# A gated-state recurrence with a mixture of experts behind it: the last chunk's first layer by 44 for 48 matmuls, the state decay as one operation, two experts of chunk 1's first half by seven products

## The chip, the cores and the metric

The kernel runs on one core of one Trainium2 chip, as one launch. The metric is the device time of an execution in microseconds (us). A core has a matrix engine (PE, TensorE; its weight loads are listed as PEld), a vector engine (DVE), an activation engine (ACT), a general engine (POOL, GpSimd) and a queue that issues transfers (SP). Each works through its own list in order. Matmuls write to PSUM, which has eight banks of 128 x 512 f32.

## The reference

```python
f = 1 / (1 + exp(-f_logit))                    # q, k, v, f_logit: 4 batches, 8 heads, 768 steps, 48 wide
for t in range(S):
    state = f[:, :, t, :, None] * state + einsum('bhd,bhe->bhde', k[:, :, t], v[:, :, t])
    y[:, :, t] = einsum('bhd,bhde->bhe', q[:, :, t], state)
x = y.transpose(0, 2, 1, 3).reshape(3072, 384)
p = domain_probs / (domain_probs.sum(-1, keepdims=True) + 1e-9)
for e in range(4):
    h = maximum(x @ w1[e], 0)                  # 384 -> 1024
    out += p[:, e:e+1] * (h @ w2[e])           # 1024 -> 384
```

## The kernel before

The 768 steps are cut into six chunks of 128 (`c` = 0 to 5). In each chunk the recurrence becomes, per batch `b`, a masked product of queries and keys plus a product with the state carried over; the chunk's 4 x 128 rows then go through the four experts. All matmuls are in bf16 with f32 sums.

**The experts.** In chunk 0 and the first half (batches 0 and 1) of chunk 1 each expert is done by itself: `add_h` makes columns of the hidden layer (`mm_h`, L492: three matmuls of 128 x 128 weights for 128 hidden columns) and `relu` takes them out of PSUM; `add_o` makes an output tile from eight matmuls of 384 columns per batch (`mm_o`, L507). From the second half of chunk 1 on, experts go in pairs `p` for two batches at a time (a half `hf`): `mm_hs` (L524, 256 columns) makes the hidden layer with the row probabilities already multiplied into x, since they are not negative, and `relu_s` (L530 on DVE, L532 on ACT) takes it out, 512 columns at a time. The second layer of a pair is done by seven products instead of eight (Strassen's scheme in Winograd's form): the hidden block is cut into 2 x 2 parts (rows by batch, columns by half), `s_sum` (L547) makes four sums of parts, `t_sum` (L569) four sums of the weights, and `mm_p` (L583) makes the seven products of eight matmuls of 192 columns. Products 1, 6, 7 and 4 are added up in one bank X, 5 and 3 in a bank Y, 2 alone in Z; after each step of X the partial result is read out, so X goes on only when the read is done (`ev_p`, L610 on DVE, copies L281 on ACT). Experts for which `BLOCKED` holds are done in the same way one by one (`mm_p1`, L591; `ev_p1`, L599); before, that is expert 1 in chunks 0 and 1.

**The state.** After each batch of a chunk but the last, `ev_kv` (L471, DVE) adds the new outer products to `Sf`, and `state` (POOL) multiplies `Sf` by the gate (L479) and casts it to bf16 (L476). The 96 state rows lie as two blocks of 48 in partitions 0 to 47 and 64 to 111, and before each block has an operation of its own: two products and two casts per batch and chunk.

**The order.** The whole program is a list of named operations. `Plan.add` gives each a rank from the table `RANKS` (one number per operation, with a letter where two engines could do it: A for ACT, D for DVE, P for POOL), and the operations are issued in the order of their ranks; each engine's list follows from that. PSUM banks and SBUF slots (`rooms`) are given out in the same order. An operation on POOL whose name begins with q, k, v, s or t (products, casts, sums) waits for the last DVE operation of that kind ahead of it in the order (`o.turn`).

Of the kernel before, what the change touches and what calls it, by code (L numbers as in the profile page):

```python
# [139 lines left out]
def kernel(  # L140
# [11 lines left out]
    nc = tc.nc  # L152
# [814 lines left out]

    for e in BLOCKED:
        t_sums(e)
# [97 lines left out]
```

## Time and profile before

| | |
|---|---|
| median of 3 runs | 288.09 us (287.63 to 289.83) |
| profiled execution | 290.13 us, its span 288.4 us, mean granted clock 0.988 |
| busy PE / PEld / DVE / ACT / POOL | 278.3 / 240.1 / 205.8 / 166.0 / 110.2 us |
| chain that ended last | PE 92%, DMA 5%, POOL 1%, SP 1% |
| transfers | 41.87 MB, mean 145 GB/s |

Busy times can't be added up: the engines work side by side. A PE that is shown as busy need not be full, since the end of a matmul is modelled with what it still takes to leave the array; how many matmuls there are in how much time says more. The chain that ended last is followed back from the last instruction, at each step to what released it; its pieces have a start, a length and the engine with the line. Rows of waits say which engine's line sat idle until which other operation ended.

### The profile page before, as it was taken

What the parts mean: (1) busy time and instruction counts of PE and PEld (TensorE: products, weight loads), DVE (VectorE), ACT (ScalarE), POOL (GpSimd) and SP (SyncE); (2) the same over time, 40 slices, a digit from 0 to 9 for tenths busy, and PEclk for the clock granted to TensorE, in tenths of its full rate; (3) what the DMA queues carried; (4) which work ended last, traced back from release to release, by engine and by line L of the source; (5) the groups of instructions that cost most, each with busy time, mean ns of one, the idle gap of its engine ahead of it and who ended that gap; (6) DMA issues with size and microseconds to landing.
All of it is one profiled execution on the core that took longest, in us unless ns stands there. A gap on an engine that the chain in (4) does not pass through costs nothing.

```text
span 288.4 us, 7572 instructions
## 1 busy us (share of the span) xinstructions
PE 278.3 (96%) x3056; PEld 240.1 (83%) x3056; DVE 205.8 (71%) x435; ACT 166.0 (58%) x326; POOL 110.2 (38%) x186
## 2 busy tenths in 40 slices
PE   6769999999999999999999999999999999999995
PEld 3549556668787998998998999998999999999995
DVE  4855576797778888856768857767578868666474
ACT  5745525848777885757768738754735434613510
POOL 5997200406496614756466552534022111000000
PEclk9977999999999999999999999999999999999999
DMA  7999999998997999989999999964930642220003
GB/s 159 199 198 208 206 193 190 188 197 163 166 174 147 200 204 187 186 165 187 209 189 185 168 203 195 172 128 91 142 91 0 97 109 55 57 56 1 30 0 113
DMA packets 153687, 41.87 MB, mean 145 GB/s; under 512 B 144028, under 2 KB 152860, under 8 KB 153652
## 3 DMA queue, kind: packets, MB, share of 16 engines
q1 hardware_dynamic: 142404, 34.66, 64.7%
q0 software_dynamic: 11248, 6.72, 16.5%
q8 instruction: 24, 0.39, 0.6%
q14 instruction: 11, 0.09, 0.1%
HBM read 31.51 MB, written 4.72 MB: 126 GB/s over the span
## 4 chain that ended last, share of the span: by engine, by line
PE 92%; DMA 5%; POOL 1%; SPq 1%; issue 0%; DVE 0%
PE ps_m L524 33%; PE ps_m L583 29%; PE ps_m L492 12%; PE ps_m L507 8%; DMA w_sb<-in_moe_w_dram 3%; PE ps_m L591 2%; PE ps_m L431 2%; PE ps_m L458 2%; DMA k<-in_k_dram 1%; PE ps_m L454 1%; PE ps_m L341 1%; PE ps_m L464 1%; POOL vb L287 1%; SPq L293 1%; PE ps_m L483 0%; PE ps_m L400 0%
## 5 line engine op out<-in xcount | busy, mean ns | idle before, releaser
L524 PE MATMUL ps_m<-x,w_sb 128*128 128x256 bf16 x864 | 107.4, 273 | 0.0
L532 ACT ACTIVATE h<-ps_m 128x512 bf16<-128x512 f32 x105 | 59.5, 602 | 63.3 <-PE ps_m L524 56.1
L524 PEld LDWEIGHTS <-w_sb 128*128 128x128 bf16 x864 | 82.3, 98 | 8.6
L583 PEld LDWEIGHTS <-S 128*128 128x128 bf16 x576 | 48.7, 98 | 1.5
L610 DVE TENSOR_TENSOR o<-ps_m,o 128x192 f32<-128x192 f32 x91 | 31.3, 353 | 23.9 <-PE ps_m L583 22.4
L492 PE MATMUL ps_m<-x,w_sb 128*128 128x128 bf16 (+2 forms) x264 | 37.5, 295 | 2.0 <-DMA w_sb<-in_moe_w_dram 2.0
L583 PEld LDWEIGHTS <-h 128*128 128x128 bf16 x432 | 36.5, 98 | 0.6
L530 DVE TENSOR_SCALAR h<-ps_m 128x512 bf16<-128x512 f32 x39 | 26.7, 687 | 12.4 <-PE ps_m L524 12.0
L414 ACT ACTIVATE yb<-ps_m,pn 128x384 bf16<-128x384 f32 x59 | 31.6, 589 | 5.3 <-PE ps_m L458 3.7
L479 POOL TENSOR_TENSOR Sf<-Sf,egs 48x192 f32<-48x192 f32 x40 | 20.2, 507 | 35.5 <-DVE S L547 18.6
L492 PEld LDWEIGHTS <-w_sb 128*128 128x128 bf16 x264 | 23.4, 105 | 10.2 <-DMA w_sb<-in_moe_w_dram 2.1
L503 ACT ACTIVATE h<-ps_m 128x512 bf16<-128x512 f32 (+1 forms) x42 | 20.8, 507 | 15.6 <-PE ps_m L492 14.6
L583 PE MATMUL ps_m<-ts_sb,S 128*128 128x192 bf16 x288 | 29.5, 246 | 0.0
L583 PE MATMUL ps_m<-w_sb,h 128*128 128x192 bf16 x288 | 29.3, 246 | 0.0
L583 PE MATMUL ps_m<-w_sb,S 128*128 128x192 bf16 x288 | 29.2, 246 | 0.0
L391 POOL TENSOR_TENSOR qk<-q,e 128x384 bf16<-128x384 f32 x19 | 22.6, 1190 | 13.8 <-issue 4.9
L547 DVE TENSOR_TENSOR S<-h 128x1024 bf16<-128x1024 bf16 x36 | 25.6, 716 | 2.9 <-ACT h L532 2.6
L507 PE MATMUL ps_m<-w_sb,h 128*128 128x384 bf16 x144 | 27.0, 326 | 0.0
L447 DVE TENSOR_TENSOR AT<-ps_m,mask 128x512 bf16<-128x512 f32 x40 | 25.6, 682 | 1.0 <-PE ps_m L431 0.9
L374 ACT ACTIVATE e<-ps_m 128x384 f32<-128x384 f32 x40 | 23.8, 713 | 3.3 <-PE ps_m L341 3.2
L476 POOL CAST sb<-Sf 48x192 bf16<-48x192 f32 x40 | 14.0, 354 | 24.8 <-DVE S L547 14.7
L391 POOL TENSOR_TENSOR qk<-k,e 128x384 bf16<-128x384 f32 x19 | 18.9, 999 | 11.7 <-PE ps_m L464 7.8
(97 smaller groups left out, 336.7 us busy)
## 6 DMA issues: line engine op xcount, KB each, us to landing
out_dram<-o SPq DMA_DIRECT2D x23, 192.0 KB, 2.5
w_sb<-in_moe_w_dram POOLq DMA_DIRECT2D x5, 768.0 KB, 17.3
q<-in_q_dram SPq DMA_DIRECT2D x10, 384.0 KB, 5.4
k<-in_k_dram SPq DMA_DIRECT2D x10, 384.0 KB, 5.2
v<-in_v_dram SPq DMA_DIRECT2D x10, 384.0 KB, 5.6
f<-in_f_logit_dram SPq DMA_DIRECT2D x9, 384.0 KB, 5.3
w_sb<-in_moe_w_dram POOLq DMA_DIRECT2D x6, 384.0 KB, 9.9
f<-in_f_logit_dram SPq DMA_DIRECT2D x6, 192.0 KB, 4.0
```

The lines of the kernel that those rows point to most:

```text
L374: nc.scalar.activation(out=o, in_=i, func=AF.Exp, scale=1.0 if j else -1.0)
L391: return engines[eng].tensor_tensor(out=tl("qk", c, b)[:, j, :, 0:D].rearrange("t (i r) d -> t i r d", r=2), in0=tl("qk"[j], c, b // 2)[:, ...
L414: nc.scalar.activation(out=ys, in_=y, func=AF.Copy, scale=pe)
L447: nc.vector.tensor_tensor(out=tl("AT", c, b)[:, r].rearrange("s i t -> s (i t)"), in0=tl("A", c, b, r).rearrange("s i t -> s (i t)"), in1= ...
L492: nc.tensor.matmul(out=hp(c, e, fc, n0, n1, nf)[:, f], lhsT=w1_sb[:, e, kk, (fc + f) * 128:(fc + f + 1) * 128], rhs=tl("xT", c)[:, kk, n0: ...
L507: nc.tensor.matmul(out=tl("op", c, e, nt)[:, 0:Din], lhsT=tl("h", c, e, half_of(c, nt * T))[:, fc, nt * T:(nt + 1) * T], rhs=w2_sb[:, e, f ...
L524: nc.tensor.matmul(out=out_[:, f], lhsT=w1_sb[:, e, kk, (fc + f) * 128:(fc + f + 1) * 128], rhs=tl("xs", c, hf, p)[:, el, kk, :], start=(k ...
L530: nc.vector.tensor_relu(out=dst, in_=tl("hp", c, hf, p, el, fc))
L532: nc.scalar.activation(out=dst, in_=tl("hp", c, hf, p, el, fc), func=AF.Relu)
L547: return nc.vector.tensor_tensor(out=o, in0=in0, in1=in1, op=op)
L583: nc.tensor.matmul(out=out_, lhsT=lhs[:, f, :], rhs=rhs[:, f, :], start=(first and el == 0 and f == 0), stop=(el == 1 and f == KH - 1), sk ...
L610: nc.vector.tensor_tensor(out=o, in0=src, in1=o, op=ALU.add)
```

## The change

1. `LOW` names all four groups (half, pair) of the last chunk. For each expert of such a group `l1_unit` makes the first layer by a seven-product scheme of its own. The first 256 of the 384 inputs by the 1024 hidden columns by the 256 rows is cut 2 x 2 x 2; the third block of 128 inputs is added to those products that end in one result each. A step makes four hidden blocks by 128 rows, 512 columns of a bank: steps 1, 6 and 7 of 4 matmuls, steps 2, 5, 3 and 4 of 8, each of 128 columns; 44 in all, where `mm_hs` has 24 of 256 columns, that is 48 such. Only the first matmul of a bank clears it. Steps 1, 6, 7, 4 share a bank X as above. Steps 2, 5 and 3 are copied by ACT into SBUF (`copy_l1`), and the hidden parts are made on DVE by an addition with a maximum against 0 (`ev_l1`), the last one on ACT alone.
2. The scheme needs five sums of first-layer weights per expert (`u_sum`) and four sums of inputs per group (`x_sum`), on DVE or POOL, in SBUF slots that the last loads have left.
3. The state decay is one operation on 112 rows (chunks 1 to 4), and decays and casts may stand on DVE or ACT too.
4. `BLOCKED` takes in expert 3 of chunk 1. In chunk 1's first half two hidden blocks of 256 columns share a bank and one eviction (`hl`).
5. `s_sum`, `s_sum1` and `t_sum` may stand on POOL. `RANKS` is new throughout.

```diff
+    def u_sum(e, j, eng):
+        a = lambda i, kk: wblk(e, i, kk)
+        in0, in1, op = {1: lambda: (a(1, 0), a(1, 1), ALU.add), 2: lambda: (usum(e, 1), a(0, 0), ALU.subtract),
+                        3: lambda: (a(0, 0), a(1, 0), ALU.subtract), 4: lambda: (a(0, 1), usum(e, 2), ALU.subtract),
+                        5: lambda: (a(0, 2), a(1, 2), ALU.subtract)}[j]()
+        return engines[eng].tensor_tensor(out=usum(e, j), in0=in0, in1=in1, op=op)
...
+        terms = {"1": lambda: [(wblk(e, 0, 0), x(0, 0))], "2": lambda: [(wblk(e, 0, 1), x(1, 0)), (wblk(e, 0, 2), x(2, 0))],
+                 "5": lambda: [(usum(e, 1), t(1)), (wblk(e, 1, 2), x(2, 1))], "6": lambda: [(usum(e, 2), t(2))],
+                 "3": lambda: [(usum(e, 4), x(1, 1)), (usum(e, 5), x(2, 1))], "7": lambda: [(usum(e, 3), t(3))],
+                 "4": lambda: [(wblk(e, 1, 1), t(4)), (wblk(e, 1, 2), x(2, 0))]}[step]()
+        out_ = tl("lp", c, hf, p, el, bank).rearrange("p (f n) -> p f n", f=KH)
+        for f in range(KH):
+            for i, (lhs, rhs) in enumerate(terms):
+                nc.tensor.matmul(out=out_[:, f], lhsT=lhs[:, f * 128:(f + 1) * 128], rhs=rhs, start=(step in "125" and f == 0 and i == 0),
+                                 stop=(i == len(terms) - 1), skip_group_check=True)
...
+        if other is None:
+            return nc.scalar.activation(out=dst, in_=src, func=AF.Relu)
+        add = tl("lc", c, hf, p, el, other).rearrange("p (f n) -> p f n", f=KH)
+        return nc.vector._custom_dve(dve_ops.TENSOR_ADD_SAT, out=dst, in0=src, in1=add, s0=float("inf"), s1=0.0)
...
+        x1 = mm("X", "1", [], 0.224)
+        z = mm("Z", "2", [], 0.447)
+        c11 = ev(0, 0, "z", [x1, cp("Z", "z", z)])
+        y5 = mm("Y", "5", [U(1), X(1)], 0.447)
+        yc = cp("Y", "y", y5)
+        x6 = mm("X", "6", [U(2), X(2), c11], 0.224)
+        y3 = mm("Y", "3", [U(4), U(5), yc], 0.447)
+        c12 = ev(0, 1, "w", [x6, cp("Y", "w", y3)])
+        x7 = mm("X", "7", [U(3), X(3), c12], 0.224)
+        c22 = ev(1, 1, "y", [x7, yc])
+        x4 = mm("X", "4", [X(4), c22], 0.447)
+        ev(1, 0, None, [x4])
...
-            for i in range(4):
-                kvdone[c, b] = P.add(f"sf {c}.{b}.{i}", {"POOL": 0.36 if i % 2 else 0.52}, lambda _, b=b, i=i: state(c, b, i // 2, i % 2), s15 + 0.2,
+            for i in ((0, 1, 3) if c else range(4)):
...
     def hl(c, e, n0, n1, xs):
-        return [(c, e, fc, n0, n1, xs) for fc in range(KF)]
+        nf = NT // (n1 - n0)
+        return [(c, e, fc, n0, n1, xs, nf) for fc in range(0, KF, nf)]
...
-BLOCKED = (1,)
+LOW = {(5, 0, 0), (5, 0, 1), (5, 1, 0), (5, 1, 1)}
+BLOCKED = {(0, 1), (1, 1), (1, 3)}
```

How the change moves instructions, at three places. First PE in the last chunk: the border between a product of the second layer and the first layer of the last chunk, before (weights `w_sb`, x, 256 columns):

```order
L583 LDWEIGHTS S_4604
L583 MATMUL ps_m_4646<-ts_sb,S_4604 128x192
L524 LDWEIGHTS w_sb
L524 MATMUL ps_m_4746<-x_4578,w_sb 128x256
L583 LDWEIGHTS S_4543
L583 MATMUL ps_m_4525<-w_sb,S_4543 128x192
```

and now (step 3 of an expert of the last group; the weight sums lie in slots called q and k, two loads alternate in a bank):

```order
L646 LDWEIGHTS h_4658
L646 MATMUL ps_m_4975<-w_sb,h_4658 128x192
L574 LDWEIGHTS q_3499
L574 MATMUL ps_m_4940<-x_4301,q_3499 128x128
L574 LDWEIGHTS k_3885
L574 MATMUL ps_m_4940<-x_4301,k_3885 128x128
L646 MATMUL ps_m_4992<-w_sb,h_4658 128x192
```

Six matmuls of 256 columns between two products have become eight of 128, with weights from two tiles in turn.

Second, the end of POOL's list, before (`qk` products, casts and decays for the last chunk are its last work):

```order
L391 TENSOR_TENSOR qk_92<-k_3139,e_106 128x8x48
L476 CAST sb<-Sf 48x4x48
L479 TENSOR_TENSOR Sf<-Sf,egs_2800 48x192
L476 CAST sb<-Sf 48x4x48
L479 TENSOR_TENSOR Sf<-Sf,egs_2798 48x192
```

and now (`v`: sums of inputs, in slots called v; `S`: sums of hidden blocks for the second layer):

```order
L486 TENSOR_TENSOR Sf<-Sf,egs_3572 112x192
L549 TENSOR_TENSOR f_3790<-w_sb 128x512
L561 TENSOR_TENSOR v_4463<-x_4301 128x256
L561 TENSOR_TENSOR x_4301<-x_4301 128x2x128
L561 TENSOR_TENSOR v_4463<-x_4301,v_4463 128x256
L610 TENSOR_TENSOR S_4896<-S_4884,h_4658 128x1024
L610 TENSOR_TENSOR S_4907<-h_4658 128x1024
L610 TENSOR_TENSOR S_5139<-h_4937,S_5081 128x1024
```

POOL, which had nothing to do in the last chunk's matmuls, now makes sums of 1024 columns that PE's products read, up to the last group.

Third, the end of SP's list, the stores, before and now:

```order
L614 DMA out_dram<-o_4095 128x384 x2
L614 DMA out_dram<-o_4797 128x192 x2
L614 DMA out_dram<-o_4505 128x384
L614 DMA out_dram<-o_4797 128x384
L614 DMA out_dram<-o_4505 128x384
```

```order
L677 DMA out_dram<-o_4681 128x384
L677 DMA out_dram<-o_4926 128x384
L677 DMA out_dram<-o_4681 128x384
L677 DMA out_dram<-o_4926 128x192 x2
```

The two stores of half a row block stood ahead of three full ones; now they are the last.

More of the change, by code (lines that the diff above doesn't have):

```diff
@@ L471, in ev_kv, with state @@
             nc.vector.tensor_tensor(out=Sf[rows, b], in0=Sf[rows, b], in1=KV[rows, :, r, :], op=ALU.add)
-    def state(c, b, r, cast):
+    def state(c, b, r, cast, eng):
         rows = slice(r * P2, r * P2 + D)
         if cast:
-            return nc.gpsimd.tensor_copy(out=Sb[rows, b, :, r * D:(r + 1) * D], in_=Sf[rows, b])
-        else:
-            eg = tl("egs", c, b)[rows, 0:NP].unsqueeze(2).broadcast_to([D, NP, D])
-            return nc.gpsimd.tensor_tensor(out=Sf[rows, b], in0=Sf[rows, b], in1=eg, op=ALU.mult)
+            return copy(eng, Sb[rows, b, :, r * D:(r + 1) * D], Sf[rows, b])
+        if c:
+            rows = slice(0, MP)
+        eg = tl("egs", c, b)[rows, 0:NP].unsqueeze(2).broadcast_to([rows.stop - rows.start, NP, D])
+        return engines[eng].tensor_tensor(out=Sf[rows, b], in0=Sf[rows, b], in1=eg, op=ALU.mult)
     def pe_xt(c, b, ks):
@@ new lines, in xsum, with x_sum @@
+    def xsum(c, hf, p, j):
+        if j == 3:
+            return tl("xs", c, hf, p)[:, :, 0, T:TH]
+        return tl("xd", c, hf)[:, p, {1: 0, 2: 1, 4: 2}[j]]
+    def x_sum(c, hf, p, j, eng):
+        x = lambda kk, r: tl("xs", c, hf, p)[:, :, kk, r * T:(r + 1) * T]
+        s = lambda i: xsum(c, hf, p, i)
+        in0, in1 = {1: lambda: (x(0, 1), x(0, 0)), 2: lambda: (x(1, 1), s(1)), 3: lambda: (x(1, 1), x(0, 1)),
+                    4: lambda: (x(1, 0), s(2))}[j]()
+        return engines[eng].tensor_tensor(out=s(j), in0=in0, in1=in1, op=ALU.subtract)
@@ L527, in relu_s, with copy_l1 @@
+    def copy_l1(c, hf, p, el, bank, to):
+        return nc.scalar.copy(out=tl("lc", c, hf, p, el, to), in_=tl("lp", c, hf, p, el, bank))
     def relu_s(c, hf, p, el, fc, eng):
@@ L568, in t_sum @@
                        3: (b(0, HI_), b(1, HI_), b(0, HI_))}[j]
[L569 removed]
+        return engines[eng].tensor_tensor(out=o, in0=in0, in1=in1, op=ALU.subtract)
     def factors(m, e, blk, s):
@@ L877, in t_sums @@
             d = [tdone[e, i] for i in {1: (), 2: (1,), 4: (2,), 3: (1,)}[j]] + wd[e, 2]
-            late_ = e not in BLOCKED and j == 3
+            late_ = (0, e) not in BLOCKED and j == 3
             if late_:
                 d += [omm[k] for k in omm if k[1] == e]
-            tdone[e, j] = P.add(f"t {e}.{j}", {"DVE": 0.56}, lambda _, j=j: t_sum(e, j), unit[0] + e if late_ else TP[e in BLOCKED], deps=d)
+            tdone[e, j] = P.add(f"t {e}.{j}", {"DVE": 0.57, "POOL": 1.65}, lambda g, j=j: t_sum(e, j, g), unit[0] + e if late_ else TP[(0, e) in BLOCKED], deps=d)
@@ new lines, with u_sums, l1_unit, mm @@
+    usums, xsums, quad = {}, {}, {}
+    def u_sums(e):
+        d = {1: (), 2: (1,), 3: (), 4: (2,), 5: ()}
+        for j in (1, 2, 3, 4, 5):
+            key = {3: ("gp", "u3", e // 2), 5: ("k", "ud", e // 2)}.get(j, ("f", "ua", e % 2) if e < 2 else ("q", "ub", e % 2))
+            usums[e, j] = P.add(f"su {e}.{j}", {"DVE": 0.43, "POOL": 1.16}, lambda g, j=j: u_sum(e, j, g), unit[0] - 20,
+                                deps=[usums[e, i] for i in d[j]] + wd[e, 1], takes=[key])
+    def l1_unit(c, hf, p, el):
+        e, pr = 2 * p + el, unit[0]
+        K = lambda bank: ("ps_m", "lp", c, hf, p, el, bank)
+        L = lambda i: ("QK", "lc", c, hf, p, el, i)
+        xd = [xdone[c, b][p] for b in (2 * hf, 2 * hf + 1)]
+        xk, hk, sk = ("x", "xs", c, hf, p), ("h", "hs", c, hf, p), ("v", "xd", c, hf)
+        if el == 0:
+            for j, dj in ((1, []), (2, [1]), (3, [1]), (4, [2])):
+                xsums[c, hf, p, j] = P.add(f"sx {c}.{hf}.{p}.{j}", {"DVE": 0.3, "POOL": 0.68}, lambda g, j=j: x_sum(c, hf, p, j, g), pr - 8,
+                                           deps=xd + [xsums[c, hf, p, i] for i in dj], takes=[sk], frees=[xk])
+        X = lambda j: xsums[c, hf, p, j]
+        U = lambda j: usums[e, j]
+        def mm(bank, step, deps, cost):
+            return P.add(f"hl {c}.{hf}.{p}.{el}.{step}", {"PE": cost}, lambda _: mm_l1(c, hf, p, el, bank, step), pr, deps=xd + wd[e, 1] + deps,
+                         takes=[K(bank)], lag=0.2, frees=[xk] + ([sk] if step in "5674" else []))
+        def cp(bank, to, dep):
+            return P.add(f"cl {c}.{hf}.{p}.{el}.{to}", {"ACT": 0.6}, lambda _: copy_l1(c, hf, p, el, bank, to), pr, deps=[dep],
+                         takes=[L(to)], frees=[K(bank)])
+        def ev(kh, r, other, deps):
+            o = P.add(f"rl {c}.{hf}.{p}.{el}.{kh}.{r}", {"ACT": 0.6} if other is None else {"DVE": 0.69},
+                      lambda _: ev_l1(c, hf, p, el, kh, r, other), pr, deps=deps, takes=[hk], frees=[K("X")] + ([L(other)] if other else []))
+            quad.setdefault((c, hf, p, kh, r), []).append(o)
+            hsd.setdefault((c, hf, p), []).append(o)
+            return o
+        x1 = mm("X", "1", [], 0.224)
[10 more added lines that the diff above has]
+        ev(1, 0, None, [x4])
@@ L940, in step @@
             unit[0] += 1
+        if hg in LOW:
+            l1_unit(*hg, 0)
+            l1_unit(*hg, 1)
+            s_units(hg)
+            todo.extend((pg, i) for i in range(7))
+            while todo:
+                step()
+            return
         if hg == TAIL:
@@ L966, in zip_groups @@
             unit[0] += 1
-    for e in BLOCKED:
+    early = [e for e in range(E) if (0, e) in BLOCKED]
+    for e in early:
         t_sums(e)
@@ L986 @@
             zip_units([], ol(0, E - 1, ALL))
+            for e in range(E):
+                if (1, e) in BLOCKED and e not in early:
+                    t_sums(e)
             zip_units(hl(c, 0, 0, N2, LO), [])
```

66 lines of the change are left out of this document (47 added, 19 removed), and 114 rows, old and new, of the table RANKS.

## The prediction

> **What bounds the kernel now.** I read the page's busy times first, then the time by stages, then what TensorE (PE) waited for, then the chain that ended last, and at the end the last microseconds of the timeline. The stages, with the columns start:end, length, and busy time and count of each engine:
>
> ```profile
> PE 278.3 (96%) x3056; PEld 240.1 (83%) x3056; DVE 205.8 (71%) x435; ACT 166.0 (58%) x326; POOL 110.2 (38%) x186
> core 0: us, PE busy (x) PEld busy (x) DVE busy (x) ACT busy (x) POOL busy (x), PEclk, DMA share, GB/s
> 0.00:28.00 28.00, 21.25 (x258) 16.23 (x259) 16.68 (x42) 16.06 (x35) 22.58 (x46) 0.88 1.21 190
> 28.00:240.00 212.00, 212.00 (x2311) 181.12 (x2309) 158.56 (x329) 133.56 (x260) 87.59 (x140) 1.00 0.92 163
> 240.00:284.90 44.90, 44.90 (x494) 42.71 (x491) 30.21 (x65) 16.35 (x32) 0.00 (x0) 1.00 0.13 32
> 284.90:288.40 3.50, 0.15 (x2) 0.00 (x0) 0.36 (x1) 0.00 (x0) 0.00 (x0) 0.98 0.45 169
> ```
>
> PE is idle only in the first 28 us (6.75 us) and behind its last matmul (3.35 us). Between them it is busy for 256.9 us out of 256.9, at granted clock 1.00. A busy PE need not be a full one, so I look at pieces of the chain that ended last (start, length, what). In it a product of eight 192-column matmuls lasts 0.66 us again and again, forty-two 256-column matmuls 4.59 us and eight 384-column ones 1.30 us, and each piece starts where the one before it ends:
>
> ```profile
> 56.28 1.30 PE ps_m L507 x8
> 258.06 1.32 PE ps_m L583 x16
> 264.64 4.59 PE ps_m L524 x42
> 269.22 1.98 PE ps_m L583 x24
> ```
>
> So PE is packed: 1.32/16 = 82.5 ns for 192 columns, 4.59/42 = 109.3 ns for 256, 1.30/8 = 162.5 ns for 384. No hidden stall is there to be recovered. The time can fall only by fewer columns through PE, by a shorter start, or by a shorter tail; it rises by any new wait of PE.
>
> **The change part by part.** The program up to the second expert's first layer (about 32 us) is issued as before, so the idle time at the start stays: 0.
>
> *Last chunk's first layer.* 192 matmuls of 256 columns go, 352 of 128 columns come (4 groups x 2 experts x 44). The columns fall by 8%, but 160 matmuls and weight loads are added, so the price of a short matmul decides. Before has 96 of them, in chunk 0, each with weights of its own:
>
> ```profile
> L492 PE MATMUL ps_m<-x,w_sb 128*128 128x128 bf16 x96 | 8.2, 253 | 2.0 <-DMA w_sb<-in_moe_w_dram 2.0
> 27.16 0.83 PE L492 MATMUL ps_m<-x,w_sb 128*128 128x128 bf16 x12
> 27.83 0.33 PE L464 MATMUL ps_m<-vb,qk 128*128 128x96 bf16 x4
> L583 PEld LDWEIGHTS <-S 128*128 128x128 bf16 x576 | 48.7, 98 | 1.5
> ```
>
> Twelve of them start at 27.16 and the next product at 27.83: 0.67/12 = 55.8 ns each. The sum: 192 x 109.3 ns = 20.98 us go, 352 x 55.8 ns = 19.64 us come, **-1.34 us**. Bounds: half of a 256-column matmul, 54.6 ns, would give -1.76; if a load of 98 ns (last row) could not be hidden behind so short a matmul, 352 x 98 ns = 34.5 us, +13.5. The 55.8 ns already contain a load per matmul, so I stay near the lower end.
>
> The Trainium skill speaks against this edit: "TensorE: Matmul & The Clock Gate", section "Back-to-back issue gap", puts a sustained stream of load and matmul at about 81 ns for 128 columns. By it this term would be 352 x 81 ns - 20.98 us, an estimate of +7.5 us; the twelve matmuls at 55.8 ns disagree, but they are a short run, so I keep it as a rival.
>
> *Expert 3 of chunk 1's first half.* 16 matmuls of 384 columns become 28 of 192: 16 x 162.5 - 28 x 82.5 ns = **-0.29 us**. Expert 1 was already done in this way.
>
> *What the other engines get.* Per expert and half of the last chunk, four evictions of 512 columns become seven (three ACT copies, three DVE additions with a maximum, one ACT maximum); 20 sums of weights and 16 of inputs are new; 36 sums of hidden blocks and 6 of the second layer's weights now stand on POOL, where before all stood on DVE; of 16 state updates one decay each is gone, and 24 casts or decays leave POOL. Rows for their prices:
>
> ```profile
> L447 DVE TENSOR_TENSOR AT<-ps_m,mask 128x512 bf16<-128x512 f32 x40 | 25.6, 682 | 1.0 <-PE ps_m L431 0.9
> L610 DVE TENSOR_TENSOR o<-ps_m,o 128x192 f32<-128x192 f32 x91 | 31.3, 353 | 23.9 <-PE ps_m L583 22.4 <-ACT o L281 0.7
> L532 ACT ACTIVATE h<-ps_m 128x512 bf16<-128x512 f32 x105 | 59.5, 602 | 63.3 <-PE ps_m L524 56.1 <-DVE h L530 3.4 <-issue 3.1
> L547 DVE TENSOR_TENSOR S<-h 128x1024 bf16<-128x1024 bf16 x36 | 25.6, 716 | 2.9 <-ACT h L532 2.6
> L391 POOL TENSOR_TENSOR qk<-k,e 128x384 bf16<-128x384 f32 x19 | 18.9, 999 | 11.7 <-PE ps_m L464 7.8 <-DVE S L547 3.8
> L391 POOL TENSOR_TENSOR qk<-q,e 128x384 bf16<-128x384 f32 x19 | 22.6, 1190 | 13.8 <-issue 4.9 <-ACT e L374 3.9 <-DVE S L547 2.8
> L282 POOL CAST vb<-v 128x384 bf16<-128x384 f32 x18 | 9.4, 526 | 11.8 <-DVE S L547 11.7
> ```
>
> The DVE addition reads 512 f32 columns of PSUM and 512 of SBUF: 0.69 us by the first row (0.68), at worst twice that. A POOL sum of 1024 columns is not in the trace: by the cast (526/384 = 1.37 ns a column) 1.40 us, by the product with k (2.60 ns) 2.66 us; two inputs, but 16-bit ones, so I take 2.1 and keep both ends.
>
> Do they keep up? From PE's first matmul of step 1 in the last chunk to its last matmul, PE has 52 short steps and 37 products, about 52 x 0.345 + 37 x 0.66 = 42.3 us. DVE has in that stretch 24 additions, 32 evictions at 0.37, 8 sums and a small one: 16.6 + 11.8 + 5.7 + 0.3 = 34.4 us. POOL has 11 sums and 8 small ones: 11 x 2.1 + 8 x 0.7 = 29 us (35 at the slow end). ACT has 21 copies, 8 maxima at 0.60 and 9 small: 20.4 us. All below 42.3.
>
> Single hand-overs. An expert's four results leave one bank one after the other, and PE must not come back to it too early. Where two steps of an expert lie closest (7 and 4 of the first expert), PE has three short steps (8, 4 and 4 matmuls) and a product between them: 0.447 + 0.224 + 0.224 + 0.66 = 1.56 us, against 0.2 us to the start of the eviction (below, the tail's rows), 0.69 for it and 0.1 back: 0.57 to spare, if no other eviction stands ahead on DVE. The second bank, emptied by ACT, has 1.32 us at the closest against 0.2 + 0.6 + 0.1. In the densest stretch of POOL (the end of chunk 2, two sums, one sum of weights and another sum in a row) the products that need the first two stand 6.6 and 8.0 us behind, against 2.1 and 4.2; with 2.66 us a sum it is 2.7 and 5.3, still covered. The last POOL sum, which the last but one product reads: its input comes 0.8 us after the last step 4, the sum ends 3.0 us (slow: 3.6) after it, and seven products (4.6 us) stand between. At the start of chunk 1, POOL's t sum has 1.9 us to spare; a product with q that POOL now makes for the first transposes is only 0.2 us ahead. I book **+0.4 us** of waits, between 0 and 2.4 (0.1 us at each of 24 hand-overs of the last chunk). Fewer, wider evictions in chunk 1's first half, and the state decay in one operation, relieve ACT, DVE and POOL, on which PE does not wait in the stages from 28 us on: 0. If that cover were gone, POOL's 16 removed decays are 16 x 0.5 = 8 us of POOL time.
>
> *Tail.* Before, the last operation is an eviction at 285.08, and then one full store:
>
> ```profile
> 284.22 0.82 PE L583 MATMUL ps_m<-w_sb,S 128*128 128x192 bf16 x8
> 285.08 0.36 DVE L610 TENSOR_TENSOR o<-ps_m,o 128x192 f32<-128x192 f32 x1 [0.30 <-PE ps_m L583]
> out_dram<-o SPq DMA_DIRECT2D x23, 192.0 KB, 2.5
> out_dram<-o SPq DMA_DIRECT2D x2, 96.0 KB, 1.7
> ```
>
> After, the two half stores of 96 KB stand last on SP's queue, so the landing behind the last eviction is 2.5 - 1.7 = 0.8 us shorter; the other half store goes out some 0.6 us earlier and may still be in its way. I take **-0.6** (0 to -0.8).
>
> Sum: -1.34 - 0.29 + 0.4 - 0.6 = -1.83 us on a span of 288.4 us (profiled execution 290.13 us, that is 2.0 above the median of the runs, 288.09). Carried over to the median: 288.09 - 1.83 = **286.2 us**. Ends of the terms without the 98 ns: -1.76 - 0.29 - 0.8 = -2.85 (285.2) and -1.34 - 0.29 + 2.4 = +0.8 (288.9).
>
> **The rivals.**
>
> *The gain is eaten by waits (no gain).* For it: three more evictions per expert, DVE at 34.4 of 42.3 us, and POOL's load up by about two thirds. Against: the spare times above. If half of the 24 hand-overs came 0.2 us late, or POOL's sums 2 us late once: -1.83 + 2.4 = 288.7 us.
>
> *POOL and DVE stand in each other's way (slower).* The kernel lets POOL's sums wait for the DVE sum before them. Before shows that a two-input operation can be held up by the other engine (least, median, longest time in ns):
>
> ```profile
> L547 DVE TENSOR_TENSOR S<-h x36: 676/684/1046, 101.5 to 279.5; 128x1024 bf16<-128x1024 bf16 x36
> L282 POOL CAST vb<-v x18: 497/502/899, 57.6 to 217.0; 128x384 bf16<-128x384 f32 x18
> ```
>
> With sums of 2 us on POOL the hold could be 2 us instead of 0.4. It decides when a POOL sum with its wait takes 4 us: then the second of the two sums at the end of chunk 2 ends at 8.0 us, just where its product stands, and the next, 6 us later, is some 3.5 us too late; two stretches as dense make +7, 288.1 - 1.8 + 7 = 293 us. Against: the medians, 684 and 502, show that most were not held. The Trainium skill, "SBUF — State Buffer", section "Who interferes with whom", has such a rule, an exclusive lock between GpSimd and a DVE operation with two SBUF inputs; the two longest times agree with it.
>
> *Short matmuls wait for their weights (slower).* The 81 ns case: between the 55.8 and the 98 ns of the rows, about half way, 352 x 77 ns is +6.1, with the other terms 293.7 us.
>
> *The addition is slower than its row.* Above (42.3 - 34.4)/24 + 0.69 = 1.02 us each, DVE becomes the bound of the last chunk; at 1.38 us it has 51 us of work against 42.3: 288.1 - 1.8 + 8.7 = 295 us.
>
> That the change is not what it says is excluded by the instruction order: 352 matmuls of 128 columns stand there, and 192 of 256 are gone.
>
> **How the numbers follow.** Forecast 0.64; no gain 0.19; POOL against DVE 0.08; weights 0.04; addition 0.05. Everything above 285.2 and below 289.5 holds the forecast nearly whole and the no-gain case; most of the 0.17 of the slow cases is left out, and nothing speaks for less than -2.85 but scatter. Range 285.0 to 289.5. Within 1% (about what a measurement can tell from no change) is 285.2 to 291.0: faster by over 1% needs all terms at their good end, 0.10; slower by over 1% is the slow cases, less their mild forms, 0.14; the rest 0.76.
>
> **What would show it.** Right: 12 short matmuls in about 0.67 us in the last chunk, PE without waits from 28 us on, PE's last matmul 1.2 us earlier, and a last store of 96 KB. Wrong: a pace of 75 ns or more on the first layer's new line; PE waiting for DVE additions or POOL sums; POOL sums above 2.7 us; additions above 1 us; PE idle time in the first 28 us other than 6.75 us.

## The result, and the profile after

The changed kernel takes **286.57 us** (median of 9 runs, 285.22 to 288.07), the kernel before 288.37 us (median of 9 runs, 287.63 to 290.55). The ratio is 0.9936, 95% interval 0.991 to 0.9961: 0.6% faster, and 286.2 us was predicted. The nine runs of the changed kernel also differ in the mean clock that was granted to PE: 285.22 to 286.96 us at 1.00 (five runs), 286.57 to 287.56 us at 0.994 (three), 288.07 us at 0.988 (one).

The two profiled executions are further apart than the medians: 290.13 us before, 285.82 us now, spans 288.4 and 284.1 us. So the span has to be cut into pieces before anything is put down to the change. From the page and from the table by stages (start:end, length, busy time and count of PE, PEld, DVE, ACT, POOL, then the clock granted to PE):

```profile
PE 276.0 (97%) x3228; PEld 241.2 (85%) x3228; DVE 208.7 (73%) x437; ACT 178.2 (63%) x350; POOL 185.3 (65%) x197
0.00:28.00 28.00, 23.70 (x291) 18.08 (x292) 18.61 (x47) 19.09 (x40) 22.95 (x44) 1.00 1.20 186
20.00:22.00 2.00, 2.00 (x44) 1.84 (x39) 1.94 (x5) 1.30 (x3) 1.98 (x4) 1.00 1.24 206
232.00:280.83 48.83, 48.83 (x712) 48.74 (x709) 35.58 (x75) 22.27 (x46) 30.09 (x22) 1.00 0.18 38
```

PE is full in the last 49 us, and in the first 28 us it is idle for 4.30 us, where it was 6.75 us before. The same two microseconds of the profile before, and in the timelines of both the first product of 384 columns, up to which PE has the same work:

```profile
20.00:22.00 2.00, 2.00 (x24) 1.61 (x22) 0.36 (x1) 0.60 (x1) 1.95 (x3) 0.50 1.24 205
31.28 0.81 PE L507 MATMUL ps_m<-w_sb,h 128*128 128x384 bf16 x4
28.00 0.81 PE L514 MATMUL ps_m<-w_sb,h 128*128 128x384 bf16 x4
```

In the first profile PE had waited 1.96 us for weights (the 2.0 on the L492 row in the prediction) and then ran at clock 0.50; in the second it did neither. That is 3.28 us at the start (31.28 - 28.00). The rest, from the timeline after (product 3 is the last but one; the last product, then the last eviction) and from the list of transfers:

```profile
279.51 0.82 PE L646 MATMUL ps_m<-w_sb,S 128*128 128x192 bf16 x8
280.17 0.82 PE L646 MATMUL ps_m<-w_sb,h 128*128 128x192 bf16 x8
281.03 0.36 DVE L673 TENSOR_TENSOR o<-ps_m,o 128x192 f32<-128x192 f32 x1 [0.30 <-PE ps_m L646]
out_dram<-o SPq DMA_DIRECT2D x2, 96.0 KB, 1.6
```

I call **PE's stretch** the time from that first product of 384 columns to the end of the last product (its start + 8 x 82.5 ns): 284.88 - 31.28 = 253.60 us before, 280.83 - 28.00 = 252.83 us after. Behind it come 3.52 us before and 3.27 us after. So the two spans differ by -3.28 (start) - 0.77 (stretch) - 0.25 (tail) = -4.30 us.

Within the stretch after, one place is not filled. The second load of f of chunk 1 lands late, ACT makes two exponentials or logarithms of it (L334, L342), and the sum over time `cs` (L347) of PE needs them:

```profile
47.24 0.84 ACT L334 ACTIVATE f<-f 128x768 f32<-128x768 f32 x1 [1.47 <-DMA f<-in_f_logit_dram]
48.11 0.84 ACT L342 ACTIVATE gp<-f 128x768 bf16<-128x768 f32 x1
49.01 0.48 PE L347 MATMUL ps_m<-gp,Ub 128*128 128x384 bf16 x2 [0.68 <-ACT gp L342]
```

The three hidden columns ahead of it end at 48.16, so PE loses 0.85 us. Without that the stretch is **251.98 us**, 1.62 us below the 253.60 of before.

### The profile page after: what moved, and what is told of

Read it like the earlier page. It is cut to its first block, busy times and chain, and to the rows that moved or that the text cites. A ratio compares the mean times of both kernels' runs of the same rounds, so it can differ in the third digit from the quotient of the medians.

```text
span 284.1 us, 8015 instructions
## 1 busy us (share of the span) xinstructions
PE 276.0 (97%) x3228; PEld 241.2 (85%) x3228; DVE 208.7 (73%) x437; ACT 178.2 (63%) x350; POOL 185.3 (65%) x197
## 4 chain that ended last, share of the span: by engine, by line
PE 84%; DMA 9%; POOL 4%; ACT 1%; DVE 1%; issue 0%; ACTq 0%; POOLq 0%
PE ps_m L646 29%; PE ps_m L531 26%; PE ps_m L574 7%; DMA w_sb<-in_moe_w_dram 7%; PE ps_m L514 6%; PE ps_m L499 4%; PE ps_m L654 2%; DMA f<-in_f_logit_dram 2%; PE ps_m L437 2%; POOL w_sb L312 2%; PE ps_m L464 1%; PE ps_m L460 1%; PE ps_m L347 1%; PE ps_m L470 1%; POOL AT L441 1%; PE ps_m L362 1%
## 5 line engine op out<-in xcount | busy, mean ns | idle before, releaser
L531 PE MATMUL ps_m<-x,w_sb 128*128 128x256 bf16 x672 | 84.3, 273 | 0.0
L531 PEld LDWEIGHTS <-w_sb 128*128 128x128 bf16 x672 | 63.6, 98 | 7.1
L595 ACT ACTIVATE h<-ps_m 128x512 bf16<-128x512 f32 x82 | 46.8, 600 | 24.1 <-PE ps_m L531 23.9
L610 POOL TENSOR_TENSOR S<-h 128x1024 bf16<-128x1024 bf16 x14 | 29.7, 2124 | 10.3 <-DVE S L610 6.3
L499 PE MATMUL ps_m<-x,w_sb 128*128 128x128 bf16 (+2 forms) x264 | 35.1, 282 | 0.0
L499 PEld LDWEIGHTS <-w_sb 128*128 128x128 bf16 x264 | 21.6, 98 | 8.1
L593 DVE TENSOR_SCALAR h<-ps_m 128x512 bf16<-128x512 f32 x30 | 20.6, 688 | 9.6 <-PE ps_m L531 8.5
L510 ACT ACTIVATE h<-ps_m 128x512 bf16<-128x512 f32 x33 | 19.1, 595 | 12.2 <-PE ps_m L499 11.8
L610 POOL TENSOR_TENSOR S<-h,S 128x1024 bf16<-128x1024 bf16 x10 | 21.2, 2124 | 4.5 <-DVE o L673 2.5
L514 PE MATMUL ps_m<-w_sb,h 128*128 128x384 bf16 x128 | 23.9, 326 | 0.0
L585 DVE CUSTOM_DVE_ANT_0 h<-ps_m,QK 128x512 bf16<-128x512 f32 x24 | 16.0, 686 | 5.1 <-PE ps_m L574 1.9
L588 ACT COPY QK<-ps_m 128x512 f32<-128x512 f32 x24 | 13.8, 588 | 8.1 <-PE ps_m L574 5.2
```

The source lines that it names most:

```text
L499: nc.tensor.matmul(out=hp(c, e, fc, n0, n1, nf)[:, f], lhsT=w1_sb[:, e, kk, (fc + f) * 128:(fc + f + 1) * 128], rhs=tl("xT", c)[:, kk, n0: ...
L514: nc.tensor.matmul(out=tl("op", c, e, nt)[:, 0:Din], lhsT=tl("h", c, e, half_of(c, nt * T))[:, fc, nt * T:(nt + 1) * T], rhs=w2_sb[:, e, f ...
L531: nc.tensor.matmul(out=out_[:, f], lhsT=w1_sb[:, e, kk, (fc + f) * 128:(fc + f + 1) * 128], rhs=tl("xs", c, hf, p)[:, el, kk, :], start=(k ...
L593: nc.vector.tensor_relu(out=dst, in_=tl("hp", c, hf, p, el, fc))
L595: nc.scalar.activation(out=dst, in_=tl("hp", c, hf, p, el, fc), func=AF.Relu)
L610: return engines[eng].tensor_tensor(out=o, in0=in0, in1=in1, op=op)
```

## The experiments

All stretches below are measured in the same way. "Bare" means without the waits that are named.

**1. The kernel before, profiled again.** Nothing is edited.

> The kernel before, profiled once more; nothing is edited. In its first profile PE waited 1.96 us for the first layer's weights and then ran at half clock for about 5 us; in the profile of the change it did neither, but waited 0.85 us at the sums of chunk 1 (cs 1.0, behind gate2) for a load of f. Theory 1: both belong to how the weights happen to land, not to the change. If this time PE comes without the wait at the weights, the first product of 384 columns starts at 28 us, the time is 287.6 to 288.1 us, and PE waits 0.6 to 0.9 us for f at the sums of chunk 1 here too. Theory 2: the change brought the wait for f. Then PE has no wait above 0.2 us there even when the start is fast. If the start is slow again, the product starts at 31.3 us, the time is about 290, and nothing is told apart.

Span 285.4 us, one run of 287.06 us, below the 287.6 to 288.1 us that was expected. This time PE came without the wait. Timeline of PE:

```profile
27.50 0.81 PE L507 MATMUL ps_m<-w_sb,h 128*128 128x384 bf16 x4
46.99 0.82 PE L591 MATMUL ps_m<-w_sb,S 128*128 128x192 bf16 x8
47.95 0.32 PE L341 MATMUL ps_m<-gp,Ub 128*128 128x384 bf16 x1
281.05 0.82 PE L583 MATMUL ps_m<-w_sb,S 128*128 128x192 bf16 x8
```

The product of L591 ends at 46.99 + 0.66 = 47.65, the sum comes at 47.95: 0.30 us lost at the same sums of chunk 1, and 0.32 us more at 60 us, ahead of a product of 384 columns that waits for its weights. The stretch is 281.71 - 27.50 = 254.21 us, bare 253.59, as in the first profile (253.60). Theory 1 holds in kind: the early start and the wait for f belong together and to both kernels. The size was smaller (0.30 where I gave 0.6 to 0.9), and the wait for weights was not named. Of the 4.3 us between the two spans, the 3.28 us of the start are not the change's.

**2. The last chunk's first layer as before.**

```diff
-LOW = {(5, 0, 0), (5, 0, 1), (5, 1, 0), (5, 1, 1)}
+LOW = set()
...
```

(`RANKS` for the last stage in the order of before.)

> The changed kernel with its last chunk's first layer by 192 matmuls of 256 columns again, in the order of the kernel before for that stage (all sums of the stage on DVE); expert 3 of chunk 1 and the state decay stay changed. Forecast's theory (the columns decide, at 55.8 ns a short matmul): the stretch from the first product of 384 columns to the end of the last product grows by 1.34 us (252.83 to 254.2 us, less or more what waits it has), the median to about 287.9 us. Rival (the three additional evictions per expert cost waits that eat the gain): the stretch grows by less than 0.7 us.

286.92 us median of 10 runs, 0.9968 of before (0.995 to 0.9985). Timeline of PE:

```profile
27.89 0.81 PE L512 MATMUL ps_m<-w_sb,h 128*128 128x384 bf16 x4
47.40 0.81 PE L497 MATMUL ps_m<-x,w_sb 128*128 128x512 bf16 x3
48.40 0.48 PE L345 MATMUL ps_m<-gp,Ub 128*128 128x384 bf16 x2 [0.19 <-DVE o L660]
280.93 0.82 PE L644 MATMUL ps_m<-w_sb,S 128*128 128x192 bf16 x8
```

The stretch is 281.59 - 27.89 = 253.70 us, with 0.35 us lost at 48.40: bare 253.35 us. That is 1.37 us above the changed kernel (251.98), where 1.34 was expected, and 0.25 us below the kernel before: what expert 3 brings (0.29 expected). The sums of this stage went back to DVE together with the first layer, but PE has no wait in the last chunk in either profile, so only the matmuls are left as a cause, and the rival (waits of the extra evictions) has nothing. The two ratios lie 0.0032 apart, 0.9 us of 288, and by their intervals it may be anything from 0 to 1.8 us; the median of 287.9 us that was expected did not come. All ten runs here have a mean granted clock of 0.998 or more. The five runs of the changed kernel for which that holds too have a median of 285.82 us, 1.1 us lower. So it is the stretch that decides here, not the median.

**3. 200 short matmuls in a row.** Ahead of the first hidden block of chunk 3:

```diff
+        if (c, hf, p, el, fc) == (3, 0, 0, 0, 0):
+            for i in range(200):
+                nc.tensor.matmul(out=out_[:, 0, 0:T], lhsT=w1_sb[:, e, i % KD, (i % 8) * 128:(i % 8 + 1) * 128],
+                                 rhs=tl("xs", c, hf, p)[:, el, i % KD, 0:T], start=True, stop=True)
```

> The changed kernel with 200 more matmuls of 128 columns, each with weights of its own, in one row without a break ahead of the first hidden block of chunk 3. Their result is written over. Forecast's theory: 55.8 ns each also in a long row, so the stretch of PE grows by 200 x 55.8 ns = 11.2 us and the time to 297.8. Rival (the 12 matmuls seen were too short a row, and a long one waits for its weights, 77 ns as priced in the prediction): +15.4 us, 302. The Trainium skill, TensorE: Matmul & The Clock Gate, section Back-to-back issue gap, has about 81 ns for a sustained row: by it +16.2 us.

297.07 us, one run. Timeline of PE, the row and what follows it, and from the table by stages the weight loads of that time:

```profile
155.44 11.33 PE L531 MATMUL ps_m<-x,w_sb 128*128 128x128 bf16 x200
166.60 1.58 PE L535 MATMUL ps_m<-x,w_sb 128*128 128x256 bf16 x13
155.00:167.00 12.00, 12.00 (x212) 11.97 (x210) 0.70 (x2) 2.36 (x5) 5.31 (x3) 1.00 0.98 157
```

(166.60 - 155.44)/200 = **55.8 ns**, with a weight load of its own for each. The stretch is 264.73 us; without four waits of 1.50 us in all, which lie ahead of the row, it is 11.25 us longer than 251.98 (11.2 expected). The two unbroken rows of the last chunk say the same. From the chain that ended last of the changed kernel:

```profile
249.36 1.56 PE ps_m L574 x28
256.68 2.68 PE ps_m L574 x48
```

2.68/48 = 55.8 ns. A load of 98 ns is hidden behind matmuls that follow one another in 55.8 ns. The Trainium skill, "TensorE: Matmul & The Clock Gate", section "Back-to-back issue gap", has about 81 ns for such a stream; these rows disagree, and the measurement decides. The figure in another section of that page, "Wait — 56ns, not 53.3ns?", 55.8 ns, agrees.

**4. The state decay as two operations.**

```diff
         if c:
-            rows = slice(0, MP)
+            for rows in (slice(0, D), slice(P2, P2 + D)):
+                eg = tl("egs", c, b)[rows, 0:NP].unsqueeze(2).broadcast_to([D, NP, D])
+                o = engines[eng].tensor_tensor(out=Sf[rows, b], in0=Sf[rows, b], in1=eg, op=ALU.mult)
+            return o
```

> The changed kernel with each state decay of chunks 1 to 4 as two operations on 48 rows again, on the engine that has the one now. Forecast's theory: off PE's path, the stretch of PE stays at 252.8 us within 0.2 (with its wait for f, if that is there), the time at 286.6; the engines that decay get 16 x 0.4 to 0.5 us more work. Rival (a late state holds up the outputs of the next chunk): the stretch grows by 0.4 us or more, with a wait of PE at L464.

285.91 us, one run; stretch 253.22 us. 0.31 us of it is the wait for f, 0.20 us a wait at 76.65, and 0.54 and 0.21 us are two new ones. Their timeline, several engines:

```profile
184.89 2.18 POOL L486 TENSOR_TENSOR Sf<-Sf,egs 48x192 f32<-48x192 f32 x4
188.11 1.19 POOL L397 TENSOR_TENSOR qk<-q,e 128x384 bf16<-128x384 f32 x1
189.34 1.19 ACT L380 ACTIVATE e<-ps_m 128x384 f32<-128x384 f32 x2 [2.15 <-POOL qk L397]
189.40 2.10 DVE L288 CAST sb<-Sf 48x192 bf16<-48x192 f32 x1
190.42 0.59 ACT L598 ACTIVATE h<-ps_m 128x512 bf16<-128x512 f32 x1
190.58 0.82 PE L649 MATMUL ps_m<-ts_sb,S 128*128 128x192 bf16 x8 [0.38 <-ACT e L380]
192.15 0.22 PE L464 MATMUL ps_m<-vb,AT 128*128 128x48 bf16 x2
```

Four decays, 2.18 us together, stand where the changed kernel has two, 0.99 us together. The products q and k behind them on POOL come later, and the exponentials of ACT wait 2.15 us for the slot that the products free (0.18 us in the changed kernel). PE goes on at 190.58, when the exponentials have ended (190.53); the eviction behind them (L598) is still under way then. The second wait comes from the same shift: the cast of the state on DVE now stands beside a POOL sum (189.26 to 191.39 us) and takes 2.10 us, the masked scores behind it end at 192.10, and the output of attention at L464, which reads them, starts at 192.15 for 191.94. Bare the stretch is 251.96, that of the changed kernel. The rival's size was right (0.4 us or more), its place only in the smaller part: 0.21 us at L464, 0.54 us at a product, behind POOL's and ACT's queues. What I booked at 0 covers 0.75 us in this order; whether the 0.20 us at 76.65 belong to it stays open.

**5 and 10. The loads of f earlier.**

```diff
-            after(ins[c, nm, b], ins["w", w_gate])
+            after(ins[c, nm, b], ins["w", w_gate - 1])
+        if (c, nm, b) == (1, "k", 0):
+            after(ins[c, nm, b], ins["w", w_gate])
```

and, in the second of the two, also

```diff
-        op.prio = int(rank.rstrip("ADP"))
+        op.prio = {"ld f1.2": 261.5}.get(op.name, int(rank.rstrip("ADP")))
```

> The changed kernel with the second load of f of chunk 1 held back by the weight block before (w 7 for w 8), and the load of k behind it by w 8. Theory (in a run with a fast start PE waits 0.3 to 0.85 us at the sums of chunk 1 for this load): no wait of PE there, the stretch from the first product of 384 columns to the end of the last product 251.9 to 252.1 us, and the median 0.3 to 0.9 us below the 286.6 of the changed kernel, so 285.7 to 286.3. Rival (the f load then takes the bandwidth of w 8, and PE waits for the weights of expert 3 instead): a wait for w_sb at 40 to 44 us, no gain or a loss.

> As e5, and the third load of f of chunk 1 (for batches 2 and 3) also one place earlier on SP's queue, ahead of v. In e5 PE's wait for the first f went from 0.85 to 0 us, and 0.5 us came in its place at the transposes of y 12 us later, behind an exponential that waited 3.4 us for this load. Theory (the loads set PE's pace there when the start is fast): no wait above 0.2 us after 28 us, the stretch 252.0 to 252.2, the median 285.3 to 286.0, below both kernels. Rival (v is then late, or DMA has no more to give): another wait of 0.3 us or more between 50 and 65 us, and a median of 286 or more.

286.06 us (6 runs, 0.9936 of before, 0.9914 to 0.9957) and 286.82 us (12 runs, 0.9964, 0.9933 to 0.9995). In the first, the wait at `cs` is gone and another comes 12 us later; the stretch is 252.51 us, bare 252.00, where 251.9 to 252.1 was expected. Timelines of PE and ACT:

```profile
48.71 0.49 PE L349 MATMUL ps_m<-gp,Ub 128*128 128x384 bf16 x2
59.61 0.84 ACT L336 ACTIVATE f<-f 128x768 f32<-128x768 f32 x1 [3.37 <-DMA f<-in_f_logit_dram]
60.88 0.34 PE L492 MATMUL ps_m<-ident,yb 128*128 128x128 bf16 x3 [0.35 <-ACT yb L287]
```

In the second that one is gone too, and v is late in its place (stretch 252.82 us, bare 252.01):

```profile
58.90 0.95 POOL L288 CAST vb<-v 128x384 bf16<-128x384 f32 x2 [4.63 <-DMA v<-in_v_dram]
59.90 0.21 PE L466 MATMUL ps_m<-vb,AT 128*128 128x48 bf16 x2 [0.65 <-DVE o L523]
```

(PE's wait is put down to the last operation by time; the output of attention needs `vb`, which POOL finished at 59.85.) The rival of the second run holds: after an early start the loads are the limit between 45 and 62 us, and an order of theirs only says which one is late. All thirteen profiles agree: where the first product of 384 columns comes at 29.0 us or before (seven), PE loses 0.3 to 1.0 us there in all, and where it comes at 29.7 us or later (six), nothing. Neither version is told apart from the changed kernel.

**6. PE kept busy until the weights come.**

```diff
-FILLER = {"cs 0.0": 6, "tpk 0.1": 4}
+FILLER = {"cs 0.0": 6, "tpk 0.1": 4, "h 0.0.0.0": 8}
```

> The changed kernel with 8 matmuls of 512 columns into a spare bank, 1.7 us, ahead of the first layer's first matmuls, where PE in some runs waits 2 us for weights and then runs at half clock for 5 us. Their result is not used. Theory (the idle time costs the clock, and that makes the spread of the runs): no stretch at clock 0.5 in any profile, all runs within 1.5 us of one another instead of 2.9 (285.2 to 288.1), the median between 286.3 and 287.5, since a fast start pays the 1.7 us less what the wait for f gives back. Rival (the spread comes from elsewhere, the loads for instance): the spread stays at about 2.9 us and the median goes up by 1.7.

286.05 us median of 12 runs, 0.9938 of before (0.9916 to 0.996). Timeline of PE and table by stages:

```profile
18.99 1.89 PE L1156 MATMUL ps_m<-S 128*128 128x512 bf16 x8
29.71 0.81 PE L514 MATMUL ps_m<-w_sb,h 128*128 128x384 bf16 x4
20.00:28.00 8.00, 8.00 (x144) 7.24 (x142) 5.02 (x16) 5.35 (x12) 7.68 (x17) 1.00 1.27 206
28.00:280.00 252.00, 252.00 (x2926) 222.26 (x2925) 189.30 (x388) 161.02 (x313) 160.68 (x151) 1.00 0.79 143
```

The stretch is 252.01 us with no wait at all, the 251.98 of the changed kernel confirmed. Eleven of the 12 runs lie between 285.38 and 286.73 (1.35 us), one at 288.15, so the spread shrinks as expected but for one run. That one has a mean granted clock of 0.994, the others 1.00; 0.994 and 0.993 are what the profiles of experiments 5 and 10 have with 3.4 us of half clock, so the filler seems not to have kept it away there (that run has no trace). The median is 0.25 us lower than the lowest I gave. Across the profiles without the filler the start goes with the wait for the first weights: without it, or with 0.2 us, the first product of 384 columns comes at 27.3 to 28.0 us, with 0.52 us of it at 27.89 (experiment 2) and 28.99 (10), with 0.54 us at 28.56 (5), with 0.81 us at 30.73 (9), with 1.7 to 2.0 us at 30.8 to 31.3. The clock makes most of it: of the 3.28 us before, 0.84 lie ahead of the first of the matmuls that wait (19.73 us, 18.89 in the profile after), 2.44 between it and the product. From the stages of the profile before, and of experiment 5, whose wait was 0.54 us:

```profile
18.00:20.00 2.00, 0.27 (x3) 0.27 (x4) 0.77 (x3) 0.58 (x1) 1.97 (x5) 0.64 1.35 198
22.00:24.00 2.00, 2.00 (x28) 2.00 (x27) 1.82 (x4) 0.48 (x1) 1.90 (x4) 0.50 1.27 205
24.00:26.00 2.00, 2.00 (x31) 2.00 (x30) 0.25 (x2) 1.31 (x3) 1.94 (x6) 0.65 1.31 203
```

```profile
18.00:20.00 2.00, 1.92 (x21) 1.73 (x23) 0.65 (x3) 0.97 (x2) 1.98 (x5) 0.52 1.27 204
20.00:22.00 2.00, 2.00 (x35) 1.80 (x32) 1.76 (x4) 0.65 (x2) 1.93 (x4) 0.63 1.24 206
```

A mean clock of 0.64 over 2 us is 1.44 us at half clock, and so on: 1.44 + 2 + 2 + 1.40 = 6.8 us before, 1.92 + 1.48 = 3.4 us in experiment 5. The Trainium skill, "TensorE: Matmul & The Clock Gate", section "What's actually happening", tells of a clock at half rate that is decided anew in free-running windows of about 3.4 us by how busy PE was: two windows and one window here, so the rows agree. The table of that section puts the fall of the clock behind an idle window of about 3.4 us; there the rows disagree, and the measurement decides: 0.54 us ahead of the weights, after other short gaps, was enough, while 0.52 us in experiment 2 cost no clock. That a window's phase decides this is the page's account; no run here shows the phase.

**7. All sums on DVE.**

```diff
+        if op.name[0] == "s" and op.name[1].isdigit():
+            rank = rank.replace("P", "D")
```

> The changed kernel with all sums of hidden blocks on DVE, none on POOL, in the same places. Forecast's theory (POOL's sums are covered, and DVE has room): DVE gets some 25 us more, is still below PE in each stage but close to it in the last chunk (35.6 + 11 x 0.7 = 43.3 us of 48.8), and the stretch of PE grows by 0 to 1.5 us. Rival of the prediction (POOL and DVE stand in each other's way and PE pays for it): the stretch gets shorter by 0.5 us or more. A third (DVE is full, the sums had to go to POOL): longer by 3 us or more.

289.47 us (6 runs, 1.0043 of before, 1.0012 to 1.0074), slower than before. Stretch 254.78 us, 2.80 above 251.98. Table by stages:

```profile
232.00:280.00 48.00, 46.62 (x672) 45.64 (x671) 40.74 (x81) 22.98 (x48) 8.09 (x11) 1.00 0.18 35
```

DVE is busy for 40.7 of 48 us, and PE loses 2.2 us at five places of the last chunk. My 0 to 1.5 us was too little, and the third theory (3 us or more) is the closest: a DVE at 85% no longer serves each hand-over in time. The rival (POOL and DVE cost PE something) is the wrong way round: with the sums in these places, POOL's are worth 2.8 us.

**8. Each DVE addition twice.** In `ev_l1` the addition with its maximum is issued a second time with the same operands.

> The changed kernel with each of the 24 DVE additions of the last chunk's first layer done twice, so 1.37 us for 0.69. The rival of the prediction put the limit at 1.02 us each: DVE then has 35.6 + 16.5 = 52.1 us of work against 48.8 us of PE, and PE would end 3 to 8 us later. If the single hand-over decides (0.57 us to spare between steps 7 and 4), the delay is 0.1 us at 8 hand-overs plus what queues on DVE: 1 to 2 us. If neither, less than 0.5 us.

293.65 us (4 runs, 1.0221 of before, 1.0181 to 1.0262). Stretch 259.91 us, 7.93 above 251.98. Table by stages, and waits of PE:

```profile
232.00:280.00 48.00, 43.38 (x612) 41.43 (x611) 43.55 (x83) 22.77 (x46) 26.78 (x21) 1.00 0.18 35
PE ps_m L574 <- DVE h L586: 4.0, 8, 1.0
```

The rival's mechanism is real: with 1.37 us an addition DVE is busy for 43.55 of 48 us, PE waits eight times for an addition, and the stretch grows by 7.9 us (the prediction had +8.7 us on top of its forecast, 295 us, for 1.38 us). It did not come to it because one addition takes 0.69 us. An addition of 1.02 us, the limit that the rival named, was not tried.

**9. Each POOL sum of 1024 columns twice.** In `s_sum` the sum is issued a second time when POOL has it.

> The changed kernel with each of the 30 sums of 1024 columns on POOL (chunk 1's second half to chunk 5) done twice, 4.25 us for 2.12. The prediction's rival on POOL and DVE decides from 4 us for a sum with its wait: the second of two sums in a row then stands where its product comes, and two dense stretches make +7 us. If that reckoning holds, the stretch of PE (252.0 us without the wait for f) grows by 5 to 9 us, with waits of PE for POOL sums at the products of the ends of chunks 2 and 3. If POOL's other work (products, casts and sums of weights behind the sums) is what comes late, the waits stand at other lines (transposes, outputs of attention) and the sum is larger, 10 us or more. If the sums have more room than reckoned, less than 3 us.

328.99 us, one run; stretch 323.62 - 30.73 = 292.89 us, 40.9 above 251.98. Waits of PE, the last product, and the longest sum on DVE with the POOL sum beside it:

```profile
PE ps_m L648 <- POOL S L612: 20.7, 9, 7.1
322.96 0.82 PE L648 MATMUL ps_m<-w_sb,h 128*128 128x192 bf16 x8
131.84 4.31 DVE L612 TENSOR_TENSOR S<-S,h 128x1024 bf16<-128x1024 bf16 x1
133.46 2.13 POOL L611 TENSOR_TENSOR S<-S,h 128x1024 bf16<-128x1024 bf16 x1
```

The mechanism (a sum of 4 us comes after its product) is there, its price is not: nearly six times the 7 us that I had for two dense stretches. POOL then carries some 64 us more work. The products wait for its sums at nine places, 20.7 us in all and up to 7.1 us at once; the rest are waits for other work on POOL, DVE and ACT, and a PE at half clock after the longest (granted clock 0.56 from 136 to 142 us). A DVE sum takes 4.31 us where 0.69 is usual: it stands beside a product (132.32 to 133.52 us) and a sum of POOL one behind the other, and ends 0.55 us after that sum.

**11. The last store whole.**

```diff
+        if (c, nt) == (C - 1, 2):
+            if cols.start:
+                return
+            cols = slice(0, Din)
```

> The changed kernel with its last two stores of 96 KB as one of 192 KB behind the last eviction, as before. By the prediction's term (landing 2.5 against 1.7 us) the end comes 0.6 to 0.8 us later: 3.3 to 3.5 us behind the end of the last eviction, for 2.71 in the changed kernel. By the two profiles (2.96 against 2.71 us) it comes 0.25 us later. If half a store takes as long as a whole one when nothing else is under way, 0.

Span 286.9 us with the last product's end at 283.33 us: 3.57 us behind PE, for 3.27 us with two half stores (the last eviction stands as far behind the last product in both, so the end comes 3.0 us after it for 2.7). The two profiles' 0.25 us holds within 0.05; the prediction's 0.6 to 0.8 does not. The other profiles bear it out: 2.97 to 3.08 us from the last eviction to the end with a whole store (before, experiments 1, 2 and 11), 2.72 to 2.84 us with halves, but for one of 3.03 (experiment 9).

## Why the prediction was right, and where not

**The first layer, -1.34 us: right.** 1.37 us by experiment 2, 55.8 ns by experiment 3. The row of twelve matmuls in the profile before was enough to price 352 of them.

**Expert 3, -0.29 us: right**, 0.25 us by the bare stretches of experiment 2 and of before.

**Waits, +0.4 us: wrong in place.** None of the 24 hand-overs of the last chunk shows a wait of PE, so the term should have been 0. The wait that is there (0.85 us) stands at 49 us, for a load. The ledger took the start as unchanged and PE's arrival at chunk 1's sums with it; what fails is "PE without waits from 28 us on". It needed the question what PE meets when it comes 3.3 us earlier, but experiment 1 shows that the kernel before meets it too, so it is no cost of the change.

**What the engines get: right in the prices, high for DVE.** Prices taken and found, and the stretch of the last chunk that the prediction reckoned with (42.3 us up to the last matmul):

```profile
L585 DVE CUSTOM_DVE_ANT_0 h<-ps_m,QK 128x512 bf16<-128x512 f32 x24 | 16.0, 686 | 5.1 <-PE ps_m L574 1.9 <-ACT h L583 1.6 <-ACT QK L588 0.9
L610 POOL TENSOR_TENSOR S<-h 128x1024 bf16<-128x1024 bf16 x14 | 29.7, 2124 | 10.3 <-DVE S L610 6.3 <-DVE f L549 1.4 <-ACT o L287 1.2
L610 DVE TENSOR_TENSOR S<-h x22: 677/688/1721, 99.2 to 274.8; 128x1024 bf16<-128x1024 bf16 x22
275.82 2.12 POOL L610 TENSOR_TENSOR S<-h,S 128x1024 bf16<-128x1024 bf16 x1 [2.51 <-DVE o L673]
238.50:280.83 42.33, 42.33 (x619) 42.27 (x616) 30.14 (x63) 18.73 (x39) 28.11 (x19) 1.00 0.20 43
```

686 ns for 0.69, 2.12 us for 2.1. In these 42.3 us DVE has 30.1 us, POOL 28.1 and ACT 18.7 (34.4, 29 and 20.4 were reckoned). The last POOL sum ends at 277.94, 1.57 us ahead of product 3 at 279.51. POOL does hold DVE up, as the rival had it: DVE sums take up to 1.72 us (from 105.38 to 107.10 us, beside a POOL sum from 104.43 to 106.55), but the median stays at 688 ns, and PE waits for none of them. POOL's sums are not held up here: all take 2.11 to 2.16 us. The Trainium skill, "SBUF — State Buffer", section "Who interferes with whom", has an exclusive lock between GpSimd and a DVE operation with two SBUF inputs. These rows agree: the DVE sum of 1.72 us ends 0.55 us after the POOL sum beside it, and so does that of 4.31 us in experiment 9.

**State decay, 0: right against the kernel before, but not for nothing.** Experiment 4 shows 0.75 us of waits that the edit keeps away in the new order.

**Tail, -0.6 us: the size was wrong.** 0.25 to 0.30 us. The term took the median landing of 23 stores (2.5 us), most of them issued amid other transfers, for that of a store that is alone at the end.

**Start, 0: right for the medians, not for the two profiles.** The sum as it came out is -1.62 (columns) - 0.25 (tail) = -1.87 us; the forecast of -1.83 rests on two terms that were off by 0.4 and 0.35 us and cancel. The medians differ by 1.80 us, and their interval allows 1.1 to 2.6 us. That the gain is not one of the start shows at equal clock: with a mean granted clock of 0.998 or more the kernel before has medians of 287.81, 287.43 and 287.78 us in the three series of the experiments, and the changed kernel 285.82 us; at 0.987 or 0.988 it is 289.60 to 290.52 against 288.07 us.

The rivals: weights, out (experiment 3); addition, out, its price near what was reckoned (8); POOL against DVE, there but off PE's path, its price reckoned far too low (9); no gain, out: the interval lies below 1.

## What to carry to other kernels

Where the bound engine is packed, count its columns at the pace of the shortest row that the profile has, and check each new hand-over; here both terms of columns came out within 0.05 us. Before two profiles are compared, align them at the first instruction that both reach with the same work done, and take the start, the stretch and the tail apart: here three quarters of the difference between two spans was a start that varies from run to run. An engine with a quarter of its time free is not spare room by itself: moving the sums from POOL back to DVE (from 73% to 85% of the last stage) cost 2.8 us.

## What the runs showed of the hardware

- A weight load of 98 ns per matmul of 128 columns costs nothing beside it over 200 in a row: 55.8 ns each.
- A wait of 1.7 to 2.0 us for the first weights, with short gaps ahead of it, went with half clock for 6.8 us in four profiles of four, one of 0.8 us did so once, and one of about 0.5 us went with half clock for 3.4 us in two profiles of three. Against the profile after (28.00) the same instruction comes 2.7 to 3.3 us later after 6.8 us of half clock, and 0.6 to 1.0 us later after 3.4 us.
- A small cast on DVE (48 x 192, 0.24 us otherwise) took 2.10 us beside a POOL sum of 2.13 us (experiment 4), and a DVE sum 4.31 us beside a product of 1.20 and a sum of 2.13 us of POOL (experiment 9): it is held until the POOL operations beside it end.
- A store of 96 KB at the end of everything lands only 0.3 us earlier than one of 192 KB (experiment 11).
